# Local and global attention with a routed expert layer: the order of the first global keys, and who clears the padded values of V

## The chip, the cores and the metric

The kernel runs on one core of a Trainium2 chip. The metric is the device time of one execution in microseconds; the kernel before has a median of 1015.91 us over three runs (1014.29 to 1016.57). A core has five engines that work side by side, each through its own queue in order: TensorE (PE in the profile: matrix products and transposes), VectorE (DVE), ScalarE (ACT), GpSimd (POOL) and SyncE (SP, which here only issues transfers). ScalarE and GpSimd issue transfers too; on those engines an issue takes its turn in the same queue as their arithmetic. Engines wait for one another, and for transfers, by semaphores.

## The reference

Eight batches, eight heads, 512 local and 32 global tokens per head, 64 values each. Global tokens attend to everything; local tokens attend to the 32 global keys and to the local keys at most 32 places away. The attention output, 4352 tokens of 512 values, goes into a layer of eight experts whose weights per token come from a softmax that is balanced in eight rounds over rows and columns.

```python
k_all = np.concatenate([k_g, k_l], axis=2)
v_all = np.concatenate([v_g, v_l], axis=2)
out_g = np.matmul(sm(scale * q_g @ k_all^T), v_all)
mask  = np.abs(pos[:, None] - pos[None, :]) <= 32
s_ll  = np.where(mask, scale * q_l @ k_l^T, -1e9)
s_l   = np.concatenate([scale * q_l @ k_g^T, s_ll], axis=-1)
out_l = np.matmul(sm(s_l), v_all)
...
logits = x @ w_gate            # P: softmax, then 8 rounds of row and column sums
for e in range(E):
    out += P[:, e:e+1] * (np.maximum(x @ w1[e], 0.0) @ w2[e])
```

(The products are abridged here; `sm` is the softmax over the last axis.)

## The kernel before

The attention runs in 32 units: a unit is one batch and two of its heads (four units to a batch). The loop at line 497 takes steps s = 0, 1, 2, ...; at each step several units are in work at different stages, and the instructions of all engines are issued in exactly the order in which the code names them. Nothing is reordered: what stands in front on an engine's queue goes first.

The stages of a unit n are:

- st_A (line 279): transposes of its keys and queries on TensorE (line 287), then copies out of PSUM: keys to kTe[n % 4] by VectorE (line 289), queries by ScalarE (line 292 into qpl for the first six units, line 296 into the block-diagonal qbd after that).
- st_B (line 299), in three parts: the scores of local queries with the local keys in reach and with the batch's 32 global keys (lines 316, 319, 321), masked and reduced by VectorE (line 326), exponentials by ScalarE (line 329). The global keys are read from kgT.
- st_D1 and st_D2 (lines 332, 342): transposes of the probabilities, and of a finished unit's output into xT.
- st_E (line 359): the probabilities times V (line 372), then the division (lines 376, 377).
- st_G1 to st_G4 (lines 382 to 431): the same for global queries, two units at a time. They read qgT, kgT and kTe.

From step 5 on, first-layer and then second-layer products of experts 0 and 1 (p_l1, line 448, and p_l2, line 462) are put between these stages. After the attention the balancing and the other six experts follow; they fill the time from about 360 us to the end and are not touched.

V has three tiles per batch parity. va holds the local V in blocks of 128 rows, 65 values per head: 64 of V, and a 1 in column 64 (Dh), which makes the sum of probabilities come out with the product. vb holds the same shifted by 64 rows. vgz holds the 32 global rows four times, padded with zeros, so that a product of 128 rows picks the right 32. The zeros and ones are set once for each parity: clear (line 247) does a block of zero rows in va and the columns of ones in va and vb; clear_z (line 253) zeroes vgz and sets its ones. Batch 0 uses the tiles of parity 0, cleared by VectorE (lines 258, 261); batch 1 those of parity 1, cleared by GpSimd (lines 273, 274). Later batches find the padding in place.

V comes by load_v (line 161): GpSimd issues the global V into a scratch in DRAM (line 167), four loads of va (lines 168, 171) and one of vb (line 174). For batches 0 and 1 the rest of vb is built on GpSimd by five copies out of va (part, lines 176 to 183). load_vz (line 157) brings the global V from the scratch into vgz, issued by SP.

Ahead of the loop stand: the loads of batch 0's first heads and of four batches' global keys and queries (load_gf, line 205, on SP's and ScalarE's queues), more loads on GpSimd, the zeros and ones, the band mask (built by GpSimd at line 265, copied by VectorE at lines 490 to 493), st_A(0), then the global keys of four batches at once (cast_g and transpose_g, lines 212 and 217: one cast of 128 rows, four transposes, one copy into kgT), then st_A(1). In the loop: qgs is cast at step 0 and transposed at step 1; batch 1's V loads stand at step 2 (line 503), with load_vz(1) behind the first of them (line 526); qbd is cleared by GpSimd at step 3 (line 509); batch 2's Q and K (line 501), expert 1's w1, the copies that build batch 1's vb, and expert 0's w2 at step 4 (line 513); keep_busy (line 482) puts three and two products of no use into steps 1 to 4.

Of the kernel before, what the change touches and what calls it, by code (L numbers as in the profile page):

```python
# [10 lines left out]
FP16 = mybir.dt.float16  # L11
# [12 lines left out]
def kernel(  # L24
# [13 lines left out]
    nc = tc.nc  # L38

    B, H, Sl, Dh = q_l.shape  # L40
    Sg = q_g.shape[2]
    D, E = moe_w_gate.shape
    F = moe_w1.shape[2]
    P = 128
# [6 lines left out]
    HP = H // 2  # L51
# [17 lines left out]
    identity = persist.tile([P, P], FP16)  # L69
# [58 lines left out]
    with ExitStack() as att:  # L128
# [4 lines left out]
        ps_tr = att.enter_context(tc.tile_pool(name="ps_tr", bufs=2, space=PSUM))  # L133
# [4 lines left out]
        kgT = att_c.tile([P, HP, B * Sg], FP16)  # L138
        qgT = att_c.tile([P, HP, B * Sg], FP16)
        qbd = [att_c.tile([P, NHB, P], FP16, name=f"qbd{i}") for i in range(2)]  # L140
        kTe = [att_c.tile([P, W + Sl + W], FP16, name=f"kTe{i}") for i in range(4)]
# [15 lines left out]
        def load_vz(b):  # L157
            for i in range(4):
                nc.sync.dma_start(out=vgz[b % 2][W * i : W * (i + 1), i, :, 0:Dh], in_=vg16[b])
# [36 lines left out]
        gst = {}  # L196
# [8 lines left out]
        def load_gf(hf, tg, f, engs):  # L205
            src = k_g if tg == "kgs" else q_g
            fv = f.rearrange("p (h d) -> p h d", h=H)
            for bb, eng in enumerate(engs):
                eng.dma_start(out=fv[W * bb : W * (bb + 1)], in_=src[4 * hf + bb].rearrange("h s d -> s h d"))
            gst[(hf, tg)] = (att_in.tile([P, H, Dh], FP16, tag=tg, name=tg, bufs=1), fv)  # L210

        def cast_g(tg):
            t, fv = gst[(0, tg)]
            nc.vector.tensor_copy(out=t, in_=fv)
            gst[(0, tg)] = t

        def transpose_g(hf, tg):
            t = gst[(hf, tg)]
            pt = ps_tr.tile([P, HP, P], FP16, tag="tr")
            for hp in range(HP):  # L220
                nc.tensor.transpose(pt[:, hp, :], t[:, 2 * hp : 2 * hp + 2, :], identity)
            dst = kgT if tg == "kgs" else qgT
            nc.vector.tensor_copy(out=dst[:, :, P * hf : P * (hf + 1)], in_=pt)

        def run(steps):
            for f in steps:
                f()
# [3 lines left out]
        f0 = ypool.tile([P, NJ, D], FP32, tag="y", name="f0")  # L231
        fh = [f0[:, t, :].rearrange("p (h s d) -> p h s d", h=2, s=NJ) for t in range(2)]
        for h in range(2):
            for t, (src, eng) in enumerate(((q_l, nc.sync), (k_l, nc.scalar))):
                eng.dma_start(out=fh[t][:, h], in_=src[0, h].rearrange("(p s) d -> p s d", s=NJ))
        load_gf(0, "kgs", f0[:, 2, :], (nc.sync, nc.scalar, nc.sync, nc.scalar))
        load_gf(0, "qgs", f0[:, 3, :], (nc.sync,) * 4)
        steps = load_qk(0, 2, 4, H)
        run(steps[0:2])
# [7 lines left out]
        def clear(i, eng):  # L247
            va, vb = vab[i]
            eng.memset(va[0:W, 0], 0.0)
            eng.memset(va[:, :, :, Dh:VW], 1.0)  # L250
            eng.memset(vb[:, :, :, Dh:VW], 1.0)

        def clear_z(i, eng):
            eng.memset(vgr[i].bitcast(mybir.dt.uint32), 0)
            for j in range(4):
                eng.memset(vgz[i][W * j : W * (j + 1), j, :, Dh:VW], 1.0)

        clear(0, nc.vector)
        for t in range(2):
            (nc.vector.tensor_copy if t else nc.scalar.copy)(out=staged[0][t][:, 0:2], in_=fh[t])  # L260
        clear_z(0, nc.vector)
        for a in range(2):
            band = mask[HB * a : HB * (a + 1), 1, 0:KW]
            for base, m, c in ((0, -1, 1), (2 * W, 1, -1)):
# [2 lines left out]
        run(steps[2:4])  # L267
        *steps, move = load_v(0)
        part = move()
        steps[0]()  # L270
        load_vz(0)
        run(steps[1:])
        clear(1, nc.gpsimd)
        clear_z(1, nc.gpsimd)

        st = {}
        NPL = 6
# [204 lines left out]
        def keep_busy(n):  # L482
            pm = ps_mm.tile([P, 512], FP32, tag="mm", name="pm")
            for i in range(n):
                nc.tensor.matmul(pm, identity, kgT[:, :, 0:P], start=True, stop=True)

        queue = []
        NU = B * HP
        st_A(0)
        nc.vector.tensor_copy(out=mask[:, 0, 0:KW], in_=mask[:, 1, 0:KW])  # L490
        nc.vector.tensor_copy(out=mask[:, 2, 0:KW], in_=mask[:, 1, 0:KW])
        nc.vector.memset(mask[:, 0, 0:W], NEG)
        nc.vector.memset(mask[:, 2, 3 * W : KW], NEG)
        cast_g("kgs")
        transpose_g(0, "kgs")
        st_A(1)
        for s in range(NU + 2):
            b, hp = divmod(s, HP)
            if s < NU and b + 1 < B:
                if hp == 0:  # L500
                    queue = load_qk(b + 1, 0, 4, H)
                if hp == 2:
                    *loads, move = load_v(b + 1)
                    queue += loads
                if hp == 3:
                    if s == 3:
                        part = move()
                        for t in qbd:
                            nc.gpsimd.memset(t, 0.0)
                    else:  # L510
                        queue = [move] + queue
                if s == 4:
                    queue += [lambda: wts.__setitem__(1, [load_w1(1)]), lambda: part(nc.gpsimd, True),
                              lambda: part(nc.gpsimd, False), lambda: wts[0].append(load_w2(0))]
                if s == 5:
                    queue += [lambda: load_g(1, "kgs"), lambda: load_g(1, "qgs")]
                if s == 7:
                    queue += [lambda: wts[1].append(load_w2(1))]
                take = 0 if s == 0 else 2 if s >= 8 and hp < 2 else len(queue)
                if s == 1:  # L520
                    queue += [lambda: part(nc.gpsimd, True), lambda: part(nc.gpsimd, False), load_first]
                    take = len(queue)
                for i, f in enumerate(queue[:take]):
                    f()
                    if s == 2 and i == 0:
                        load_vz(1)
                queue = queue[take:]

            if 8 <= s < 8 + 4 * (E - 2):
                sums_load(s - 8)  # L530
            if 8 < s <= 8 + 4 * (E - 2):
                sums_form(s - 9)

            l1, l2 = [], []
            if s >= 5:
                pieces = range(4 * (s - 6) + 2, 4 * (s - 6) + 6)
                l1 = [(i // FT % 2, i // FT // 2, i % FT) if i >= 0 else None for i in pieces]
            if s >= 6:
                k, hf = divmod(s - 6, 2)
                if k >= 1:  # L540
                    l2 = [((k - 1) % 2, (k - 1) // 2, 2 * hf + i) for i in range(2)]
            n1 = n2 = 0

            def f1(eng):
                nonlocal n1
                if n1 < len(l1):
                    if l1[n1]:
                        p_l1(*l1[n1], eng)
                    n1 += 1

            def f2(eng):
                nonlocal n2
                if n2 < len(l2):
                    p_l2(*l2[n2], eng)
                    n2 += 1

            g_odd = s % 2 == 1 and 3 <= s <= NU + 1
            if g_odd:
                gb, gg = divmod((s - 3) // 2, 2)
            even = s % 2 == 0 and 2 <= s <= NU  # L560
            f1("a")
            if s < NU:
                st_B(s, 0)
            if even:
                st_G1(*divmod((s - 2) // 2, 2))
            if 1 <= s <= NU:
                st_D1(s - 1)
            if s == 3:
                st_E(1)
            if g_odd:  # L570
                st_G2(gb, gg)
            f2("a")
            if s < 7:
                st_B(s, 1)
            if 1 <= s < 5:
                keep_busy(3)
            if 1 <= s:
                st_D2(s - 1 if s <= NU else None, s - 2 if s >= 4 else 0 if s == 3 else None)
            if 7 <= s < NU:
                st_B(s, 1)  # L580
            f1("a")
            if 0 < s < 7:
                st_A(s + 1)
            if s == 4:
                st_D2(None, 1)
            if s == 0:
                cast_g("qgs")
            if s == 1:
                transpose_g(0, "qgs")
            f1("v")  # L590
            if s < NU:
                st_B(s, 2)
            if s + 1 < NU and s >= 7:
                st_A(s + 1)
            if s == 2:
                st_E(0)
            if 3 <= s <= NU:
                st_E(s - 1)
            f2("a")
            if s >= 6 and (s - 6) % 4 == 0:  # L600
                logits(NJ * ((s - 6) // 4), NJ)
            if g_odd:
                st_G3(gb, gg)
            if s == 8:
                transpose_g(1, "kgs")
                transpose_g(1, "qgs")
            if s == 18:
                st_G4(0)
            f1("v")
            if 1 <= s < 5:  # L610
                keep_busy(2)
# [451 lines left out]
```

## Time and profile before

| | us |
|---|---|
| median of three runs | 1015.91 (1014.29 to 1016.57) |
| the profiled execution | 1014.09 |
| its span, first instruction to last | 1012.3 |
| TensorE busy in the span | 992.0 |
| VectorE busy | 778.9 |
| ScalarE busy | 632.7 |
| GpSimd busy | 299.7 |

The profile is of one execution. Times in a timeline count from the start of the span. "Busy" leaves out issuing instructions and waits; a row of a timeline gives the start, the duration, the engine, the line, the operation, the tile written and the tiles read, and in square brackets how long the engine was idle ahead of it and what released it. The share by engine in the chain tells which work, followed back from the last instruction, each step waited for. The granted clock is 0.999 of full speed over the whole span.

The transfer engines are busy in nearly all of the first 60 us: their mean share in the first ten fortieths of the span is 90% or more.

### The profile page before, as it was taken

How to read it: one execution, taken by the hardware profiler on the slowest of the kernel's cores; microseconds unless marked ns; L12 is line 12 of the kernel's file. 1: busy time of each engine (PE TensorE's matmuls, PEld its weight loads, DVE VectorE, ACT ScalarE, POOL GpSimd, SP SyncE). 2: the span in 40 equal slices, each digit the busy share in tenths (PEclk: the TensorE clock that was granted, in tenths of full speed). 3: DMA queues.
4: the chain of work that ended last, by engine and by line, in shares of the span. 5: the costliest groups of instructions: out<-in, count | busy, mean ns of one | idle time of the engine just before them, and what ended most of it. 6: DMA issues, size and time to landing. Idle time of an engine off the chain costs nothing.

```text
span 1012.3 us, 22271 instructions
## 1 busy us (share of the span) xinstructions
PE 992.0 (98%) x8774; PEld 644.2 (64%) x8774; DVE 778.9 (77%) x1890; ACT 632.7 (63%) x1342; POOL 299.7 (30%) x364
## 2 busy tenths in 40 slices
PE   6899999999999999999999999999999999999998
PEld 4666566656565555666666666676767676766764
DVE  7876766666664664889999888997889999887885
ACT  5877777777774566765555555556765555555551
POOL 9658878868860112111111111111111111100000
PEclk9999999999999999999999999999999999999999
DMA  9999999979952297654443333565664533123043
GB/s 164 183 164 206 223 211 214 219 162 225 224 155 84 88 256 167 157 146 115 115 115 74 73 73 74 126 186 148 158 147 121 115 74 86 48 69 74 1 105 125
DMA packets 135881, 138.40 MB, mean 137 GB/s; under 512 B 54432, under 2 KB 107872, under 8 KB 133728
## 3 DMA queue, kind: packets, MB, share of 16 engines
q0 software_dynamic: 105696, 87.32, 49.6%
q1 hardware_dynamic: 29248, 49.28, 15.0%
q8 instruction: 68, 1.11, 0.4%
q10 hardware_dynamic: 832, 0.39, 0.1%
q14 instruction: 37, 0.30, 0.1%
HBM read 144.20 MB, written 39.58 MB: 182 GB/s over the span
## 4 chain that ended last, share of the span: by engine, by line
PE 94%; DVE 3%; ACT 1%; DMA 1%; issue 0%; ACTq 0%; DVEq 0%
PE z L787 29%; PE pa L882 17%; PE ph L455 12%; PE py L469 12%; PE pb L882 9%; PE pc L882 5%; PE po L372 1%; PE zp L853 1%; PE ptw L338 1%; PE sc L319 1%; PE pk L287 1%; DVE ms L326 1%; PE po L416 1%; PE tgx L348 1%; PE pq L287 1%; DMA f<-in_k_g_dram 1%
## 5 line engine op out<-in xcount | busy, mean ns | idle before, releaser
L787 PEld LDWEIGHTS <-hs 128*128 128x128 f16 x2264 | 220.8, 98 | 92.8 <-issue 1.1
L787 PE MATMUL z<-w2e,hs 128*128 128x256 f16 x1304 | 195.6, 273 | 0.9 <-DVE oy L821 0.9
L787 PE MATMUL z<-v,hs 128*128 128x256 f16 x960 | 144.0, 273 | 0.0
L455 PE MATMUL ph<-xT,w1e 128*128 128x512 f16 (+1 forms) x576 | 129.6, 367 | 2.0 <-DVE lg L444 1.4
L469 PE MATMUL py<-w2e,hT 128*128 128x512 f16 x544 | 128.2, 379 | 0.4 <-DVE hT L460 0.4
L808 ACT COPY z<-z 128x256 f32<-128x256 f32 x98 | 35.0, 357 | 141.7 <-PE z L787 141.7
L882 PEld LDWEIGHTS <-w1e 128*128 128x128 f16 x960 | 86.5, 97 | 57.4 <-issue 1.2
L882 PE MATMUL pa<-t,s 128*128 128x512 f16 x384 | 114.2, 379 | 0.2 <-ACT s L907 0.2
L703 POOL DMA_DIRECT2D w1e<-in_moe_w_dram x24 | 17.4, 732 | 303.8 <-PE pa L882 229.9
L329 ACT ACTIVATE Pu<-ms,mx 128x160 f16<-128x160 f32 x256 | 92.2, 424 | 19.3 <-DVE mx L326 16.6
L821 DVE SCALAR_TENSOR_TENSOR oy<-z,lg,oy 128x512 f32<-128x512 f32 x128 | 95.8, 749 | 7.4 <-ACT oy L826 5.2
L783 DVE TENSOR_TENSOR hs<-hs 128x512 f16<-128x512 f16 x224 | 94.9, 424 | 8.2
L886 DVE CUSTOM_DVE_ANT_0 hx<-pb,s 128x512 f16<-128x512 f32 x96 | 65.9, 687 | 39.7 <-ACT s L916 31.5
L326 DVE CUSTOM_DVE_ANT_0 ms<-sc,mask 128x160 f32<-128x160 f32 x256 | 70.0, 320 | 34.1 <-PE sc L321 32.4
L703 POOL DMA_DIRECT2D w2e<-in_moe_w_dram x24 | 19.8, 830 | 242.6 <-PE z L787 212.3
L898 ACT ACTIVATE hs<-pc 128x512 f16<-128x512 f32 x96 | 57.2, 596 | 52.7 <-PE pc L882 52.6
L455 PEld LDWEIGHTS <-w1e 128*128 128x128 f16 x576 | 53.9, 98 | 52.6 <-issue 2.9
L886 DVE CUSTOM_DVE_ANT_0 hs<-pb,s 128x512 f16<-128x512 f32 x96 | 65.9, 686 | 27.3 <-ACT s L916 26.9
L882 PEld LDWEIGHTS <-s 128*128 128x128 f16 x720 | 65.6, 98 | 29.9 <-issue 1.8
L469 PEld LDWEIGHTS <-hT 128*128 128x128 f16 x544 | 50.0, 98 | 51.9 <-issue 0.5
L460 DVE TENSOR_SCALAR hT<-ph 128x512 f16<-128x512 f32 x58 | 40.1, 692 | 47.7 <-PE ph L455 46.4
L916 ACT COPY s<-pa 128x512 f32<-128x512 f32 x102 | 59.8, 586 | 12.0 <-PE pa L882 0.7
(194 smaller groups left out, 1968.4 us busy)
## 6 DMA issues: line engine op xcount, KB each, us to landing
ys<-yd SPq DMA_DIRECT2D x68, 256.0 KB, 3.3
yd<-yst SPq DMA_DIRECT2D x16, 1024.0 KB, 5.7
pw<-in_moe_w_dram POOLq DMA_DIRECT2D x24, 512.0 KB, 10.0
kept<-psum POOLq DMA_DIRECT2D x24, 512.0 KB, 4.8
s<-kept POOLq DMA_DIRECT2D x12, 768.0 KB, 9.1
v<-kept POOLq DMA_DIRECT2D x12, 768.0 KB, 9.1
w1e<-in_moe_w_dram POOLq DMA_DIRECT2D x12, 512.0 KB, 5.5
w2e<-in_moe_w_dram POOLq DMA_DIRECT2D x12, 512.0 KB, 6.6
```

The source lines that it names most:

```text
L326: nc.vector.tensor_tensor_reduce(out=ms[:, ii, :], in0=sc[:, SW * ii : SW * (ii + 1)], in1=mask[:, mi, :], scale=-scale, scalar=BIG, op0=A ...
L329: nc.scalar.activation(out=d["Pu"][:, i, :], in_=ms[:, ii, :], func=AF.Exp, scale=-1.0, bias=d["mx"][:, i : i + 1])
L455: nc.tensor.matmul(ph[:, 0:n], wts[e][0][:, dk, P * fm : P * (fm + 1)], xT[:, dk, c0 : c0 + n], start=(dk == 0), stop=(dk == DP - 1))
L460: nc.vector.tensor_scalar(out=hT[:, fm, 0:n], in0=ph[:, 0:n], scalar1=0.0, scalar2=None, op0=ALU.max)
L469: nc.tensor.matmul(py, hT[:, fk, P * c : P * (c + 1)], wts[e][1][:, fk, :], start=(fk == 0), stop=(fk == FT - 1))
L783: nc.vector.tensor_tensor(out=o, in0=x, in1=y, op=op)
L787: nc.tensor.matmul(o, lhs[:, fk, :], rhs[:, fk, :], start=(first and fk == 0), stop=(fk == HF - 1), skip_group_check=True)
L821: nc.vector.scalar_tensor_tensor(out=o, in0=z, scalar=p, in1=o, op0=ALU.mult, op1=ALU.add)
L882: nc.tensor.matmul(o, lhs[:, dk, P * f : P * (f + 1)], rhs[:, dk], start=(first and n == 0 and dk == 0), stop=(dk == HD - 1), skip_group_c ...
L886: nc.vector._custom_dve(TENSOR_ADD_SAT, out=self.to(i, j), in0=self.of(ps), in1=self.of(s), s0=BIG, s1=0.0)
L898: nc.scalar.activation(out=self.to(0, 0), in_=self.of(self.pc), func=AF.Relu)
L916: nc.scalar.copy(out=self.pre3, in_=self.pa)
```

## The change

It has four parts.

1. The first scores need the global keys of batch 0 alone. A new function, first_keys, casts and transposes only those 32 rows, behind st_A(0) and ahead of the loop. The cast and the transposes of the whole kgs tile move to step 2 and fill only the remaining columns of kgT (transpose_g has a start column c0); those of qgs both stand at step 1. One of the four loads of global keys goes from ScalarE's queue to SP's.
2. The second unit's transposes and copies, st_A(1), move from ahead of the loop into step 0, behind the second part of its scores.
3. The copies of the mask move ahead of st_A(0). keep_busy reads kTe[0] instead of kgT, in the same shape.
4. clear_z(0) goes from VectorE to GpSimd, behind all loads of batch 0's V, with load_vz(0) behind it. clear(1), clear_z(1) and load_vz(1) go from ahead of the loop, and from the first of batch 1's V loads, to behind all of batch 1's V loads at step 2.

```diff
+        def first_keys():
+            t, fv = gst[(0, "kgs")]
+            nc.vector.tensor_copy(out=t[0:Sg], in_=fv[0:Sg])
+            pt = ps_tr.tile([P, HP, Sg], FP16, tag="tr")
+            for hp in range(HP):
+                nc.tensor.transpose(pt[:, hp, :], t[0:Sg, 2 * hp : 2 * hp + 2, :], identity[0:Sg, 0:Sg])
+            nc.vector.tensor_copy(out=kgT[:, :, 0:Sg], in_=pt)
-        def transpose_g(hf, tg):
+        def transpose_g(hf, tg, c0=0):
...
-            nc.vector.tensor_copy(out=dst[:, :, P * hf : P * (hf + 1)], in_=pt)
+            nc.vector.tensor_copy(out=dst[:, :, P * hf + c0 : P * (hf + 1)], in_=pt[:, :, c0:P])
...
-        load_gf(0, "kgs", f0[:, 2, :], (nc.sync, nc.scalar, nc.sync, nc.scalar))
+        load_gf(0, "kgs", f0[:, 2, :], (nc.sync, nc.scalar, nc.sync, nc.sync))
...
-        clear_z(0, nc.vector)
...
-        steps[0]()
+        run(steps)
+        clear_z(0, nc.gpsimd)
         load_vz(0)
-        run(steps[1:])
-        clear(1, nc.gpsimd)
-        clear_z(1, nc.gpsimd)
...
-                nc.tensor.matmul(pm, identity, kgT[:, :, 0:P], start=True, stop=True)
+                nc.tensor.matmul(pm, identity, kTe[0][:, 0:512], start=True, stop=True)
...
-        st_A(0)
         (four copies and memsets of the mask)
-        cast_g("kgs")
-        transpose_g(0, "kgs")
-        st_A(1)
+        st_A(0)
+        first_keys()
...
                 for i, f in enumerate(queue[:take]):
                     f()
-                    if s == 2 and i == 0:
-                        load_vz(1)
+                if s == 2:
+                    clear(1, nc.gpsimd)
+                    clear_z(1, nc.gpsimd)
+                    load_vz(1)
...
-            if 0 < s < 7:
+            if s < 7:
                 st_A(s + 1)
...
-            if s == 0:
-                cast_g("qgs")
-            if s == 1:
-                transpose_g(0, "qgs")
+            if s == 1 or s == 2:
+                cast_g("qgs" if s == 1 else "kgs")
+                transpose_g(0, *(("qgs",) if s == 1 else ("kgs", Sg)))
```

## The prediction

> **What bounds the kernel now.** I read the page first (busy shares, the chain that ended last), then the timeline of the first 60 us engine by engine, since the diff touches nothing later, then the landings of single loads, and last the order of the built programs.
>
> ```profile
> span 1012.3 us, 22271 instructions
> PE 992.0 (98%) x8774; PEld 644.2 (64%) x8774; DVE 778.9 (77%) x1890; ACT 632.7 (63%) x1342; POOL 299.7 (30%) x364
> PE 94%; DVE 3%; ACT 1%; DMA 1%; issue 0%; ACTq 0%; DVEq 0%
> ```
>
> The page: TensorE sets the end. From about 42 us on it rarely waits, and then only on work that TensorE itself has just released (scores, VectorE, transposes). So a delay of TensorE at 42 us reaches the end whole; a gain ahead of 42 us reaches it only if nothing at 42 us holds TensorE back.
>
> ```profile
> 4.93 0.93 DVE L254 MEMSET vgz<- 128x1040 uint32 x1 [0.16 <-issue]
> 8.41 0.61 PE L221 MATMUL pt<-identity,kgs 128*128 128x128 f16 x4 [2.52 <-DVE kgs L214]
> 9.94 0.31 PE L316 MATMUL sc<-kTe,qpl 64*64 64x128 f16 x2
> 14.55 1.46 PE L485 MATMUL pm<-kgT,identity 128*128 128x512 f16 x3
> 20.37 0.82 PE L485 MATMUL pm<-kgT,identity 128*128 128x512 f16 x3
> 42.00 0.22 PE L372 MATMUL po<-va,pw 128*64 128x65 f16 x1
> 42.01 0.22 PE L372 MATMUL po<-vb,pw 128*64 128x65 f16 x1
> 42.63 0.62 PE L416 MATMUL po<-vb,pgs 128*128 128x260 f16 x4
> ```
>
> TensorE's timeline (the first line is VectorE's): the first scores start at 9.94, behind the global keys and the second unit's transposes. At 42.00 stands st_E(4), the first reader of batch 1's va, vb and vgz; it runs without a wait. The two pm rows are equal work, at 14.55 and at 20.37, with different prices: TensorE is slow until somewhere between 16.2 and 17.9.
>
> ```profile
> 10.47 0.52 POOL L249 MEMSET va<- 32x520 f16 x1
> 11.05 0.24 POOL L250 MEMSET va<- 128x32 f16 x1
> 11.11 0.33 POOL L251 MEMSET vb<- 128x32 f16 x1
> 11.17 1.13 POOL L254 MEMSET vgz<- 128x1040 uint32 x1
> 12.36 0.83 POOL L256 MEMSET vgz<- 32x8 f16 x4
> 13.10 0.76 POOL L153 DMA_DIRECT2D qs<-in_q_l_dram  x1
> ...
> 25.93 0.61 POOL L174 DMA_DIRECT2D vb<-in_v_l_dram  x1
> 26.57 1.85 POOL L509 MEMSET qbd<- 128x1024 f16 x2
> 30.46 0.76 POOL L153 DMA_DIRECT2D qs<-in_q_l_dram  x1 [2.03 <-PE po L417]
> ...
> 34.23 0.61 POOL L178 COPY vb<-va 32x520 f16<-32x520 f16 x1
> ...
> 38.00 0.61 POOL L183 COPY vb<-va 64x520 f16<-64x520 f16 x1
> ```
>
> ```profile
> L174 POOL DMA_DIRECT2D vb<-in_v_l_dram x1: 607/607/607, 25.9 to 25.9; - x1
> DMA to landing us min/median/max: 8.6/8.6/8.6
> ```
>
> GpSimd's timeline and the landing of batch 1's last load of V. GpSimd's queue runs in order and holds, one behind another, batch 1's V loads (to 26.5), the clearing of qbd, batch 2's Q and K loads, w1e(1), and the five copies that build batch 1's vb, which end at 38.61. The V load issued at 25.93 lands 8.6 later, at 34.5; the va load issued at 25.0 lands by 34.3. The clears of batch 1's padded values ran from 10.47 to 13.1, long before those loads, and nothing on GpSimd stands still for V: the copies come to their turn at 34.23.
>
> **The change part by part.**
>
> *Start.* VectorE loses clear_z(0) ahead of the first scores (4.93 to 6.45). Its queue becomes: ks cast ends 4.77; four mask copies, 0.51 from 7.09 to 7.60, so to 5.3; kTe(0) copy when its transposes end (4.82 + 0.64 = 5.46), to 6.2; cast of batch 0's k_g. That load landed 4.4 after its issue at 1.66, at 6.1 (the four k_g: 4.4 to 5.5), so the cast (0.49, its free size is unchanged) ends at 6.7. The narrow transposes and copy have no row; from above the wide ones (0.61 + 0.42), from below nothing: scores at 6.7 to 7.8. I take 7.8, the nearest row: 2.1 earlier than 9.94. If k_g landed with the late ones (5.5), 1.1 of it is gone.
>
> *What pays that back.* st_A(1) now sits inside step 0: VectorE's kTe copy 0.69 enters between the scores, the qgs cast 0.45 leaves: +0.24 on VectorE; ScalarE's qpl copy 0.48 enters there too, and ScalarE's row of eleven exponentials (11.02 to 14.64) is the longer queue, so I count +0.5. Step 1: qgs cast ahead of its transposes, +0.45. Step 2: kgs cast 0.45, four transposes 0.41, copy 0.3 to 0.42, all ahead of VectorE's last two scores: +1.2. Together +2.15 against -2.1: at 42 us nothing is won, with bounds of -1.3 (the late casts hidden under other waits) and +1.1 (k_g late).
>
> *At nothing.* One k_g load goes from ScalarE's queue to SP's: one issue of 0.45, the q_g loads behind it are wanted only in step 1; ScalarE's next work waits for q_l anyway. keep_busy reads kTe[0] in the same shape (0.82 for three); st_A(4) rewrites kTe[0] only behind it. clear_z(0) on GpSimd takes 1.93 (11.17 to 13.10) where clear(1) and clear_z(1) took 2.63, so batch 1's Q and K are issued 0.7 earlier; load_vz(0) on SP waits for it until about 12.4 instead of 12.0. st_E(0) reads it at 22.8; these loads took 4.5 to 9.5. Without that slack a late vgz(0) would hold TensorE 1:1.
>
> *The clears of batch 1.* They go behind batch 1's V loads on the same queue. They write the ones columns of the very tiles that those loads fill, and in the order of the built program the second one (va's ones) waits for the four va loads and the third (vb's ones) for the vb load: the tracking does not see that columns 0 to 63 and 64 are apart. In the program before, these memsets wait for no load. So GpSimd stands from about 26 until 34.5 with everything behind it: vgz(1), qbd, four Q/K loads of batch 2, w1e(1), the copies to vb, w2e(0), the second kgs and qgs, V of batch 2; SP's load_vz(1) waits for it as well. By rows: vb's ones start at 34.53; from there to the end of clear_z, 11.11 to 13.10, 1.99: 36.52; qbd 1.85: 38.37; the next load at 38.4 instead of 30.46: all behind it is 7.94 later. (The 2.03 idle ahead of 30.46 is swallowed; its releaser was at 30.4.) L183 then ends at 46.55 instead of 38.61.
>
> st_E(4) wants that copy at its third column block, half way through its 32 matmuls, about 42.28. In-order TensorE stands there until 46.55: +4.27. If V lands 0.7 earlier, as the earlier issue would allow at best, +3.6; the loads were queued behind w1e(0) and Q/K, so not all 0.7 arrives. I take **+4.0**. A gain at the start doesn't alter it, since the 46.55 comes from loads and GpSimd alone: the start is worth 0 on this path, whatever it saves.
>
> Late next: load_vz(1) starts near 36.5 instead of 30.5; issue 2 plus 4.5 to 9.5 gives 43 to 48; its longest landing was one sent while w1e(1) was moving, and now nothing moves between 34.5 and 38.4, so I take it inside the 46.5. w1e(1) landed at 45.5 for a first use past 55.8; w2e(0) at 50.5 for 62.4; batch 2's vb at 68 for st_E(8) near 77. All have over 9 for a delay of 8, with TensorE itself 4 later: cost 0.
>
> Sum against the profiled execution (1014.09: span 1012.3 and 1.8 around it): 1014.09 + 4.0 = 1018.1. The median of the three runs lies 1.8 above that execution, so forecast **1019.9**.
>
> *A rule that could make it worse.* The row: three pm cost 1.46 at 14.55 and 0.82 at 20.37, a ratio of 1.78, and no idle of TensorE past 10 us exceeds 1.02, so the trace can't show what 4 us of idle does. The Trainium skill, TensorE: Matmul & The Clock Gate, section "What's actually happening", says that TensorE falls to half its clock after one idle window of about 3.4 us; the slow rows at the start agree, the fall no row here shows. By that rule the sum would be the first rival's 1022.4, without it 1019.9.
>
> **The rivals.**
>
> 1. *TensorE comes out of the stall slow.* It would idle 4 to 5 us. Behind st_E(4) the chain is TensorE's back to back from 42.6 to 45.4, then mostly VectorE to 47.3, then TensorE to 50.0. At 1.78 the first 2.8 cost 2.2 more, the next 2.7 another 2.1 if it stays slow that long (at the start it stayed slow some 8 us of work, from 8.4). With 2.5 to the forecast: 1022.4, to 1024 at worst. For: the two pm prices. Against: no row shows TensorE falling back once it is fast, though none has an idle a quarter as long. Chance 0.25.
>
> 2. *The clears don't hold st_E(4), and the start's gain stays: faster.* Place: va's and vb's ones on GpSimd. It decides if batch 1's V lands by 30.3 or GpSimd catches up 4 us. For: batch 0's V landed 7.0 after issue. Against: 8.6 to 9.3 here, and the queue behind is packed. Then 1015.9 - 2.1 = 1013.8. Chance 0.06.
>
> 3. *Half hidden: no change to tell.* V lands some 2 us earlier, as the four vgz(1) loads, which fell among it at 30.5 to 34.3, are gone, and a bit of the start's gain counts: +0 to +2, say 1017. Chance 0.08.
>
> **How the numbers follow.** Forecast (+3.2 to +4.8) 0.61, rival 1 0.25, rival 2 0.06, rival 3 0.08. About 0.2% (2.0 us) is what a measurement of this kernel can tell from no change. Faster 0.06, same 0.08, slower 0.86. The range leaves out rivals 2 and 3 and the end of rival 1: 1017.0 to 1023.0.
>
> **What would show it.** GpSimd's timeline: idle of some 8 us ahead of va's ones, released by a DMA of va or vb; L178's copies near 42 to 46.6. TensorE: an idle of about 4 us inside st_E(4), ended by GpSimd's vb. First scores near 7.8, but st_E(4) reached near 42. Rival 1: the first-layer matmuls (L455 before) right behind st_E(4) far above 1.9 for eight. Wrong if GpSimd shows no such idle, or if the copies end before st_E(4).

## The result and the profile after

The changed kernel is slower by about half a percent: 1019.52 us median of six runs (1017.82 to 1021.48) against 1014.71 (1013.75 to 1016.57) for the kernel before, also of six, taken beside it. The ratio is 1.0045 with a 95% interval of 1.0029 to 1.0060, so 2.9 to 6.1 us. The forecast was 1019.9 us. Its way to that number holds only in part, and the runs below show where. One execution, of a kernel of experiment 5, ran at a granted clock of 0.657 and took 1464.71 us; it is in no time and no ratio below.

The profiled execution of the changed kernel took 1019.63 us. Its page, the span, the busy times and the shares of the chain by engine:

```profile
span 1017.9 us, 22281 instructions
...
PE 994.7 (98%) x8778; PEld 645.4 (63%) x8778; DVE 779.2 (77%) x1887; ACT 633.3 (62%) x1342; POOL 301.6 (30%) x369
...
PE 94%; DVE 4%; ACT 1%; issue 1%; DMA 0%; ACTq 0%; DVEq 0%
```

TensorE is still the bound; the span grew by 5.6 us and its busy time by only 2.7. GpSimd's timeline around batch 1's V (start, duration, engine, line, operation, tiles; in brackets the idle time ahead and what ended it):

```profile
25.84 0.52 POOL L257 MEMSET va<- 32x520 f16 x1
33.34 0.25 POOL L258 MEMSET va<- 128x32 f16 x1 [6.98 <-DMA va<-in_v_l_dram]
33.46 0.28 POOL L259 MEMSET vb<- 128x32 f16 x1
...
35.38 1.85 POOL L512 MEMSET qbd<- 128x1024 f16 x2
37.16 0.76 POOL L153 DMA_DIRECT2D qs<-in_q_l_dram  x1
...
40.94 0.61 POOL L178 COPY vb<-va 32x520 f16<-32x520 f16 x1
...
44.71 0.62 POOL L183 COPY vb<-va 64x520 f16<-64x520 f16 x1
```

The landing of that last V load (issued at 25.17, so it was there at 33.4):

```profile
L174 POOL DMA_DIRECT2D vb<-in_v_l_dram x1: 625/625/625, 25.2 to 25.2; - x1
...
DMA to landing us min/median/max: 8.2/8.2/8.2
```

The predicted stop is there, 6.98 us ahead of va's ones and ended by a load of va; batch 2's loads are issued from 37.16 instead of 30.46, and the last copy into vb ends at 45.33 instead of 38.61, 6.7 later. TensorE's timeline of the same execution:

```profile
6.77 0.31 PE L321 MATMUL sc<-kTe,qpl 64*64 64x128 f16 x2
...
7.16 0.23 PE L321 MATMUL sc<-kgT,qpl 64*64 64x32 f16 x2
...
20.93 1.46 PE L490 MATMUL pm<-kTe,identity 128*128 128x512 f16 x3
...
24.65 0.40 PE L229 MATMUL pt<-identity,kgs 128*128 128x128 f16 x4 [1.35 <-DVE kgs L214]
...
46.05 0.22 PE L377 MATMUL po<-va,pw 128*64 128x65 f16 x1
46.05 0.22 PE L377 MATMUL po<-vb,pw 128*64 128x65 f16 x1
...
47.24 1.89 PE L460 MATMUL ph<-xT,w1e 128*128 128x512 f16 x8
```

The first scores start at 6.77 instead of 9.94. But st_E(4) is reached at 46.05, and no bracket stands at it: TensorE found vb ready, because it was itself 4.05 late (42.00 before). That is not what was forecast. Three of keep_busy's products (pm) still cost 1.46 at 20.93, where before they cost 0.82 at 20.37; TensorE stayed slow until about 22.6, and the kgs cast that step 2 now holds met it with another wait. Two copies on VectorE then came beside GpSimd's late clearing of qbd (35.38 to 37.23):

```profile
35.92 1.39 DVE L340 COPY Pl<-Pu 128x256 f16<-128x256 f16 x1
36.05 1.26 DVE L345 COPY pw<-ptw 128x1024 f16<-128x1024 f16 x1
```

The same two copies in the kernel before, and, in a second view, TensorE's first-layer products behind its st_E(4) and the scores that follow them:

```profile
32.94 0.56 DVE L335 COPY Pl<-Pu 128x256 f16<-128x256 f16 x1
33.08 0.68 DVE L340 COPY pw<-ptw 128x1024 f16<-128x1024 f16 x1
```

```profile
43.20 1.89 PE L455 MATMUL ph<-xT,w1e 128*128 128x512 f16 x8
44.92 0.22 PE L319 MATMUL sc<-kTe,qbd 128*128 128x128 f16 x1
```

So this execution was 2.98 late when the copies began, 3.81 late when the first ended and 3.55 when the second did. The question for the experiments was therefore whether the clears cost the time at all, or the start does.

### The profile page after: what moved, and what is told of

Read it like the earlier page. It is cut to its first block, busy times and chain, and to the rows that moved or that the text cites. A ratio compares the mean times of both kernels' runs of the same rounds, so it can differ in the third digit from the quotient of the medians.

```text
span 1017.9 us, 22281 instructions
## 1 busy us (share of the span) xinstructions
PE 994.7 (98%) x8778; PEld 645.4 (63%) x8778; DVE 779.2 (77%) x1887; ACT 633.3 (62%) x1342; POOL 301.6 (30%) x369
## 4 chain that ended last, share of the span: by engine, by line
PE 94%; DVE 4%; ACT 1%; issue 1%; DMA 0%; ACTq 0%; DVEq 0%
PE z L791 29%; PE pa L886 17%; PE ph L460 12%; PE py L474 11%; PE pb L886 9%; PE pc L886 5%; PE po L377 1%; PE zp L857 1%; PE sc L324 1%; PE ptw L343 1%; PE pk L292 1%; DVE ms L331 1%; DVE Pl L340 1%; PE tgx L353 1%; PE po L421 1%
```

## The experiments

All kernels compute the whole output; where products of no use are added, they only take time. Each time stands beside runs of the kernel before on the same chip.

**1. The start alone, the clears alone.** The first kernel is the changed one with batch 1's clears and load_vz(1) put back where they were:

```diff
         load_vz(0)
+        clear(1, nc.gpsimd)
+        clear_z(1, nc.gpsimd)
...
-                if s == 2:
-                    clear(1, nc.gpsimd)
-                    clear_z(1, nc.gpsimd)
-                    load_vz(1)
+                    if s == 2 and i == 0:
+                        load_vz(1)
```

> The changed kernel with the clears of batch 1 and load_vz(1) back where they were (ahead of the loop; behind the first load of batch 1's V). Two theories. Hold: GpSimd's stop for batch 1's V costs the 4.8 us, as forecast; without it the time is that of the kernel before, 1014.7, at most 1 us more. Start: the stop is hidden behind TensorE, which comes to st_E(4) at 46.0 by itself; only VectorE's two copies that ran beside GpSimd's clearing of qbd (0.7 late) and beside the vb copies (0.4) are won: st_E(4) near 45, 1017.5 to 1019, slower than before by 0.3 to 0.4%.

The second is the kernel before with nothing but the late clears:

```diff
-        clear(1, nc.gpsimd)
-        clear_z(1, nc.gpsimd)
...
-                    if s == 2 and i == 0:
-                        load_vz(1)
+                if s == 2:
+                    clear(1, nc.gpsimd)
+                    clear_z(1, nc.gpsimd)
+                    load_vz(1)
```

> The kernel before with one thing changed: the clears of batch 1 and load_vz(1) behind batch 1's loads of V. Hold: GpSimd stops for 7 to 8 us, the last copy of vb ends near 45 instead of 38.6, and TensorE, which was at st_E(4) at 42.0, stands there for about 3: +3, near 1017.7. If a late GpSimd costs nothing anywhere: +0 to +0.5, near 1015. Both theories of the first run agree with +3 here; only a chain through VectorE (copies beside the clearing of qbd, +1) could make st_E(4) late by itself.

The start alone: 1016.22 us (12 runs) against 1015.14, ratio 1.0011 [0.9999, 1.0024]. The clears alone: 1020.02 (6 runs), ratio 1.0050 [1.0037, 1.0063]. So the late clears carry all of the loss, in an order whose start is that of before. GpSimd's and TensorE's timelines of the kernel with the clears alone:

```profile
32.69 0.25 POOL L250 MEMSET va<- 128x32 f16 x1 [7.05 <-DMA va<-in_v_l_dram]
...
44.05 0.62 POOL L183 COPY vb<-va 64x520 f16<-64x520 f16 x1
```

```profile
41.30 0.22 PE L370 MATMUL po<-va,pw 128*64 128x65 f16 x1
44.16 0.19 PE L370 MATMUL po<-vb,pw 128*64 128x65 f16 x1 [2.63 <-POOL vb L182]
...
45.22 1.05 PE L414 MATMUL po<-vb,pgs 128*128 128x260 f16 x4
46.06 0.43 PE L415 MATMUL po<-vgz,pgs 128*128 128x260 f16 x1
46.28 2.85 PE L453 MATMUL ph<-xT,w1e 128*128 128x512 f16 x8
```

Here TensorE does stand inside st_E(4), for 2.63 us, until GpSimd's copy into vb (line 182; line 183 is met next, at 44.72). And behind it, it is slow: 1.05 for four products that took 0.62 before, 2.85 for eight that took 1.89. The granted clock (PEclk) of the same execution shows it, in stretches of 3.41 us:

```profile
core 0: us, PE busy (x) PEld busy (x) DVE busy (x) ACT busy (x) POOL busy (x), PEclk, DMA share, GB/s
41.39:44.80 3.41, 0.66 (x22) 0.43 (x24) 0.92 (x5) 1.10 (x3) 3.35 (x5) 1.00 1.27 162
44.81:48.22 3.41, 3.41 (x25) 1.84 (x25) 1.61 (x5) 0.61 (x2) 3.41 (x6) 0.50 1.14 210
48.23:51.64 3.41, 2.81 (x43) 1.91 (x42) 2.79 (x11) 2.06 (x5) 0.72 (x2) 1.00 1.18 208
```

TensorE ran at half clock from 44.81 to 48.22. The expected 1017.7 had the wait and not this, and was 2.3 us too low. In the kernel with the start alone nothing waits there:

```profile
41.77 0.22 PE L379 MATMUL po<-va,pw 128*64 128x65 f16 x1
...
42.40 0.62 PE L423 MATMUL po<-vb,pgs 128*128 128x260 f16 x4
...
42.96 1.89 PE L462 MATMUL ph<-xT,w1e 128*128 128x512 f16 x8
```

It reaches st_E(4) at 41.77 instead of 42.00, though its scores began 3 us earlier.

**2. The changed kernel once more.** If the route of the first profile (slow start, no wait) was that execution's and not the order's, a second profile of the unchanged kernel can show the other route.

> The changed kernel once more, one look. In its first profile TensorE stayed slow until 22.6, st_E(4) was reached at 46.05 and found the last copy of vb done at 45.3. Hold: the slow stretch is chance; where TensorE becomes fast earlier, it comes to st_E(4) near 42 and is stopped there until GpSimd's copies end near 45, and the end is the same, 1018 to 1020. Start: the slow stretch belongs to the changed order; TensorE is slow until 22 again and st_E(4) is reached at 46 without a stop.

It took 1019.94 us beside 1015.1. TensorE's timeline of this second execution:

```profile
17.04 0.60 PE L490 MATMUL pm<-kTe,identity 128*128 128x512 f16 x2
...
41.54 0.22 PE L377 MATMUL po<-va,pw 128*64 128x65 f16 x1
45.12 0.19 PE L377 MATMUL po<-vb,pw 128*64 128x65 f16 x1 [3.37 <-POOL vb L182]
...
45.69 0.21 PE L377 MATMUL po<-vb,pw 128*64 128x65 f16 x1
...
46.22 1.05 PE L421 MATMUL po<-vb,pgs 128*128 128x260 f16 x4
47.06 0.43 PE L422 MATMUL po<-vgz,pgs 128*128 128x260 f16 x1
47.28 2.61 PE L460 MATMUL ph<-xT,w1e 128*128 128x512 f16 x8
49.73 0.22 PE L324 MATMUL sc<-kTe,qbd 128*128 128x128 f16 x1
```

The two pm products at 17.04 cost 0.60 (1.03 at 17.24 in the first profile), so the same program became fast some 8 us earlier. It then reached st_E(4) at 41.54 and was held 3.37 us, as forecast, and came out slow (granted clock 0.50 from 45.32 to 48.74). Two executions of one order take two routes to nearly the same lateness: one loses the time at the start and meets a vb that is ready, the other is on time and waits for it. A route without a wait in one profile was no evidence that GpSimd cost nothing. How often an execution takes which route is not known from two profiles.

**3. What TensorE's speed behind the stop costs.** Twelve products of no use right ahead of st_E(4) keep TensorE at work for most of the stop:

```diff
+            if s == 5:
+                keep_busy(12)
             if 3 <= s <= NU:
                 st_E(s - 1)
```

> The changed kernel with twelve products of no use (128x512) right ahead of st_E(4), so that TensorE works through most of the stop there. In the second look at the changed kernel TensorE waited 3.4 at st_E(4), and then eight first-layer products took 2.61 instead of 1.89 and the value products 1.0 instead of 0.6. If TensorE falls back to slow because it stood still, it stays fast here: the eight products take 1.9, and the time is 1 to 2 us below the changed kernel, near 1018. If the slow stretch has another cause, 1019.5 to 1020.5.

```profile
41.28 2.76 PE L490 MATMUL pm<-kTe,identity 128*128 128x512 f16 x12
43.98 0.22 PE L377 MATMUL po<-va,pw 128*64 128x65 f16 x1
45.49 0.19 PE L377 MATMUL po<-vb,pw 128*64 128x65 f16 x1 [1.29 <-POOL vb L182]
...
46.40 0.62 PE L421 MATMUL po<-vb,pgs 128*128 128x260 f16 x4
...
46.97 1.89 PE L460 MATMUL ph<-xT,w1e 128*128 128x512 f16 x8
```

TensorE's timeline of this kernel: 1.29 us of idle is left, and the products behind it have the prices of before. The granted clock reads 1.00 from 41 to 50 us. The place is settled; on the whole time, where 1 to 2 us less were expected, it could not be told: 1019.35 (6 runs) against 1015.33, ratio 1.0041 [1.0026, 1.0056]. Its copies into vb also ended later in the profiled execution (fifth vb product at 46.05, against 45.69 in the second profile), which took back part of what the speed gave.

**4. Which clear makes the stop.** Only the zeros and ones of va and vb go back ahead of the loop; clear_z(1) and load_vz(1) stay late:

```diff
         load_vz(0)
+        clear(1, nc.gpsimd)
...
                 if s == 2:
-                    clear(1, nc.gpsimd)
                     clear_z(1, nc.gpsimd)
                     load_vz(1)
```

> The changed kernel with clear(1) alone back ahead of the loop; clear_z(1) and load_vz(1) stay behind batch 1's loads of V. The memsets of the ones then wait for no load, and GpSimd does not stop, though the work of clear_z(1) stays where the change put it. If the stop is the cause: GpSimd's copies end at 38 to 40, as before, no stop at st_E(4), 1014.5 to 1016.5 as in the first run. If the place of the work is the cause, waits or not: 1018 and more.

1015.80 (12 runs), ratio 1.0003 [0.9988, 1.0018]. GpSimd's timeline has no idle for V, and the chain behind it is early again:

```profile
26.66 0.97 POOL L262 MEMSET vgz<- 128x1040 uint32 x1
...
28.42 1.85 POOL L513 MEMSET qbd<- 128x1024 f16 x2
...
38.41 0.62 POOL L183 COPY vb<-va 64x520 f16<-64x520 f16 x1
```

TensorE's timeline shows what is late next once vb is not:

```profile
43.92 0.19 PE L378 MATMUL po<-vgz,pg 128*64 128x65 f16 x1 [1.13 <-DMA vgz<-vg]
```

This is load_vz(1), which stands behind clear_z(1). The unit's next scores come at 46.66 (44.92 before), and the lateness of 1.74 is still there at 78.38 (76.64 before). The interval of the whole time reaches to 1.0018, 1.8 us, so it neither shows nor excludes this. To take the wait of the ones away without moving them was not tried.

**5. Whether the start can be made to pay.** Four kernels tried to turn 3 us of earlier scores into time. The first fills TensorE's idle time in steps 0 to 2 of the start-alone kernel with products of no use:

```diff
             if s == 1 or s == 2:
+                keep_busy(2 if s == 1 else 4)
                 cast_g("qgs" if s == 1 else "kgs")
...
-            if 1 <= s < 5:
+            if s < 5:
                 keep_busy(2)
```

> The first run's kernel with products of no use in TensorE's waits: two at the end of step 0, two ahead of the cast of qgs in step 1, four ahead of the cast of kgs in step 2. In the changed kernel TensorE is slow until about 22.5 (three pm products 1.46 at 20.93), in the kernel before until about 17. If the waits in steps 0 to 2 keep it slow, it is fast by 18 here and st_E(4) comes 1.5 to 2 us earlier than in the first run: near 1016. If the waits have no part in it, the same as the first run or up to 0.5 later.

1015.82 (11 runs), ratio 1.0004 [0.9992, 1.0015]; no profile of it is read. The next are the kernel before, the changed kernel and the start-alone kernel with 30 small products of no use ahead of st_A(0) (the kernel before has 20 more behind it):

```diff
+        def warm(n):
+            pm = ps_mm.tile([P, 512], FP32, tag="mm", name="pm")
+            for i in range(n):
+                nc.tensor.matmul(pm[:, 0:P], identity, identity, start=True, stop=True)
+
+        warm(30)
         st_A(0)
```

> The kernel before with products of no use of the identity in TensorE's idle start: 30 ahead of st_A(0), 20 behind it. If steady work makes TensorE fast, it is fast by 10 instead of 17: the three pm products of step 1 take 0.82 instead of 1.46, and st_E(3) comes 1 to 2 us earlier. st_E(4) also waits for the last load of vgz(1), which landed at 42.0 in the kernel before, so the gain may stop there: 1013 to 1014.7. If work doesn't matter: 1014.7.

> The changed kernel with 30 products of the identity, of no use, ahead of st_A(0), which make TensorE fast from the start. Hold: TensorE comes to st_E(4) at 40 to 41.5, stops there until GpSimd's copies of vb end at 45 or a little later, and the time stays at 1018 to 1019.5. Start: with the slow stretch gone the loss is gone, 1014.5 to 1016.

> The first run's kernel (clears of batch 1 ahead of the loop) with the same 30 products. Both theories: no stop, TensorE fast throughout, st_E(4) at 40 to 41, 1013 to 1015, and less spread than the first run's 1014.2 to 1018.4, if that spread came from when TensorE became fast. If the spread has another source, it stays.

The kernel before with them: 1013.93, ratio 1.0001 [0.9983, 1.0019], with three of its twelve runs near 1020 (1019.85 to 1020.18); the changed kernel: 1021.89, 1.0058 [1.0039, 1.0076], above the expected range, and with st_E(4) reached no earlier than before (42.62); the start-alone kernel: 1015.86, 1.0009 [0.9993, 1.0025]. The last has not less spread than without the products (1014.25 to 1021.74, against 1014.18 to 1018.40), so the spread is not shown to come from the start. In the warmed kernel before the three pm products cost 0.82 at 14.20, as was meant. To see whether its runs near 1020 come again, it was run once more.

> The kernel before with products of the identity, of no use, ahead of st_A(0) (30) and behind it (20), once more, to see whether its three runs near 1020 of twelve come again. If they are its own: 1013.9 with some runs near 1020; if they were the chip's: 1013 to 1015 throughout.

1014.81, ratio 0.9997 [0.9986, 1.0008], the slowest of twelve runs at 1018.29. TensorE's row for the three pm products, first of the one execution and then of the other:

```profile
14.20 0.82 PE L485 MATMUL pm<-kgT,identity 128*128 128x512 f16 x3
```

```profile
14.45 1.46 PE L485 MATMUL pm<-kgT,identity 128*128 128x512 f16 x3
```

The same instructions, once fast and once slow: the early products make TensorE fast, but do not keep it so. In the slow one the granted clock falls to 0.50 at 11.06 and returns at 17.89; in the fast one it reads 1.00 throughout. In the other two warmed kernels it is 0.50 from 9.44 to 19.68 (changed; the three products cost 1.46 at 12.57) and from 7.76 to 14.59 (start alone; 1.46 at 12.37), though no idle time above 0.93 us lay between the 30 products and the fall.

The last takes away what would be late next in the start-alone kernel: batch 1's global V is loaded right behind batch 0's V, and load_vz(1) follows at once.

```diff
-                nc.gpsimd.dma_start(out=vg16[b], in_=v_g[b].rearrange("h g d -> g h d"))
+                if b != 1:
+                    nc.gpsimd.dma_start(out=vg16[b], in_=v_g[b].rearrange("h g d -> g h d"))
...
         clear(1, nc.gpsimd)
         clear_z(1, nc.gpsimd)
+        nc.gpsimd.dma_start(out=vg16[1], in_=v_g[1].rearrange("h g d -> g h d"))
+        load_vz(1)
...
-                    if s == 2 and i == 0:
-                        load_vz(1)
```

> The first run's kernel (clears of batch 1 ahead) with batch 1's global V loaded behind batch 0's V and vgz(1) filled at once, instead of behind expert 0's w1. In the run with only the ones ahead, st_E(4) waited 1.1 for vgz(1); in the one with the warm start 1.7. If that load is what TensorE meets next, no wait for vgz here, st_E(4) at 41.5 to 42: 1014 to 1015, below the first run's 1016.2. If it seldom decides, the same as the first run.

1016.50 (11 runs), ratio 1.0002 [0.9993, 1.0012]; st_E(4) is reached at 41.91 with nothing to wait for, but the time is not below that of the start alone, as it was expected to be. So no form of the start gained time that could be measured, and no kernel beats the kernel before. Nor does time won by 77 us have to reach the end: in the fast profile of the warmed kernel before the scores near 77 start at 75.61, 1.03 early, and its span is 1012.1, 0.2 shorter.

**All of them at four marks.** The starts of the same instructions on TensorE: the fifth vb product of st_E(4), which is the first that needs line 183's copy; the scores behind the eight first-layer products; the same scores three units on. "Behind the stop" is the second mark less the first, less the 2.64 (44.92 - 42.28) of before.

| kernel | st_E(4) reached | wait for vb | fifth vb product | scores | late | behind the stop | scores near 77 | late |
|---|---|---|---|---|---|---|---|---|
| before | 42.00 | 0 | 42.28 | 44.92 | | | 76.64 | |
| changed, first profile | 46.05 | 0 | 46.33 | 48.97 | 4.05 | 0 | 80.68 | 4.04 |
| changed, second profile | 41.54 | 3.37 | 45.69 | 49.73 | 4.81 | 1.40 | 81.44 | 4.80 |
| clears alone | 41.30 | 2.63 | 44.72 | 48.97 | 4.05 | 1.61 | 80.68 | 4.04 |
| changed, warmed | 42.62 | 2.87 | 46.27 | 50.60 | 5.68 | 1.69 | 82.31 | 5.67 |
| changed, stop filled | 43.98 | 1.29 | 46.05 | 48.69 | 3.77 | 0 | 80.41 | 3.77 |
| start alone | 41.77 | 0 | 42.05 | 44.69 | -0.23 | 0 | 76.40 | -0.24 |
| start alone, early global V | 41.91 | 0 | 42.19 | 44.83 | -0.09 | 0 | 76.55 | -0.09 |

What TensorE is late at 45 us it is late at 77, to 0.01 us. And the measured times divide by the stop: kernels whose GpSimd stops for V have ratios of 1.0041 and more, those without the stop 1.0011 and less. The lateness is not the whole growth of a profile, though. Against 1012.3 before, the spans of the five profiles with the stop are 5.0 to 7.7 longer, 1.0 to 2.0 more than their lateness near 77; those of the start alone, with early global V, and with the ones ahead are 0.4, 0.6 and 1.6 longer, which is 0.6 and 0.7 more and 0.1 less. No run was made to find what adds this behind 77 us.

## Why the prediction was right, and where it was wrong

*The bound, and that a delay at 42 us reaches the end whole: right.* The columns "late" at 45 and 77 us agree in every kernel, and no profile with the stop makes up for its lateness later. The difference of the medians, 1019.52 - 1014.71 = 4.81, is the size of the lateness in the second profile; that both are the same to the hundredth is chance, since more is added behind 77 us.

*The stop of GpSimd: right in place and cause, over in size.* The ones of va wait for the loads of va. The prediction had GpSimd back at 34.5; it was back at 33.34 (32.69 with the clears alone). V was issued 0.76 earlier (25.17 instead of 25.93) and landed after 8.2 instead of 8.6. The prediction saw the earlier issue and let it count for 0.27 of the 4.27; a shorter landing stands only in its rival 3. From vb's ones to the end of line 183's copy it reckoned 12.02 (34.53 to 46.55); 11.87 was measured (33.46 to 45.33). So the term that was mis-sized is the landing of V, by 1.1.

*The hold of TensorE, +4.0: too high.* Where TensorE was held (second profile), the fifth vb product came 45.69 - 42.28 = 3.41 late. TensorE had come 0.46 early (41.54), stood 3.37 for line 182's copy, and then shortly for line 183's. In the first profile the copies ended (45.33) before st_E(4) was reached (46.05): that is the sign by which the prediction would have been wrong, and there the lateness came by the other route.

*TensorE comes out fast: this step failed.* The forecast counted nothing for it and gave the slow exit to rival 1, with 2.5 us. It came out slow in all three profiled executions that were held 2.63 us or more, for 1.40, 1.61 and 1.69 us; with 1.29 us of idle time it came out fast. So rival 1's mechanism is part of the true cause, at 0.56 to 0.68 of its price: TensorE had half its clock for 3.41 us in each of the three, then the old prices. Half of 3.41 is 1.71, and up to 1.69 of it was lost; the rival reckoned with slow prices for longer. The first profile, where nothing was held, shows the other side: eight products at 1.89. The forecast's total is near because misses offset. By the second profile the hold was 0.6 less than +4.0, the slow exit 1.4 more than nothing, and the median of before, taken at 1015.91 from three runs, was 1014.71 over six, 1.2 less. Together -0.6 + 1.4 - 1.2 = -0.4: 1019.5 instead of 1019.9. That it comes out so near is luck: the first profile has neither of the first two terms, and the sum leaves out what is added behind 77 us.

The rule that was weighed there, from the Trainium skill, TensorE: Matmul & The Clock Gate, section "What's actually happening", is that TensorE drops to half its clock after an idle window of about 3.4 us. The fall itself agrees with the rows (granted clock 0.50; four products 1.05 instead of 0.62). The length does not, read as one unbroken idle stretch: 2.63 us was enough here, and the measurement decides. Nor were the 3.41 us ahead of the fall free of work: TensorE was busy for 0.66, 0.18 and 1.15 us of them. The page adds that the window runs freely and that the moment of warming varies from run to run, by 500 ns either way; the two executions of one program, fast some 8 us apart, agree that it varies, but by far more.

*The start, worth 0: right.* Its two terms stand in the start-alone kernel: scores about 3 us earlier, st_E(4) at 41.77, 0.23 earlier, within the bounds of -1.3 to +1.1, and no measurable gain at the end. The narrow transposes and their copy took 0.28 and 0.23, where the wide ones' 0.61 and 0.42 were taken; the gain was 2.96 instead of 2.1 (scores at 6.98) and the payback 2.73 instead of 2.15. In the first profile of the changed kernel, though, the start was not worth 0: that execution was 2.98 late when the two copies began, ahead of any read of vb.

*Late next, at nothing: right for the changed kernel, and only behind the stop.* load_vz(1) was not met in either profile. With the stop gone it is next, for 1.13 us in the kernel with the ones ahead.

*Rivals 2 and 3* (the clears hidden, or half hidden) are refuted by the kernel with the clears alone, at 1.0050.

*What stays open.* Why TensorE stayed slow until 22.6 in the first profile, beyond that it is the execution and not the order. In that profile the span is 5.6 longer but TensorE only 4.04 late at 77 us: the other 1.5 arises between 90 and 121 us, and no run was made for it; the six runs of the changed kernel spread over 3.7 us.

## What to carry to other kernels

A memset of padding columns into a tile that a load is filling can wait for the whole load, even where the bytes are apart; put it ahead of the load's issue, or look up its waits in the built order before putting it behind. Count what stands behind the waiting instruction on its queue, not the instruction: here a memset of 0.25 us held 12 us of GpSimd's work. And take a second profile of the same program before believing that a chain without a wait clears a suspect: where two routes to the same lateness run in parallel, one execution shows only one of them.

## What the hardware showed unexpectedly

Behind a stop TensorE ran at half clock for the same 3.41 us each time: the granted clock is 0.50 from 44.81 to 48.22 (clears alone), 45.32 to 48.74 (second profile) and 46.99 to 50.40 (changed, warmed), and 1.00 on both sides. It fell not at the end of the wait but 0.2 to 1.3 us behind it, so the first products behind the stop still had the old prices (the first two rounds of st_E(4) in the second profile, 0.19 to 0.22 each, against mostly 0.24 and 0.25 from 45.31 on). The length of a single idle time does not decide it: 2.63 us was enough, 1.29 was not, nor the 1.72 for which the warmed start-alone kernel waits for vgz (clock 1.00 from 41 to 50 us); but early in two warmed kernels it fell with no idle time above 0.93 us. What does decide it these runs don't show. At the very start the column of the granted clock reads 1.00 while equal products are slow (1.46 at 20.93 in the first profile), so there only the prices show it.

A copy on VectorE was held by GpSimd's two memsets of qbd in the first profile. Line 340's, which reads and writes SBUF, took 1.39 instead of 0.56 and ended at 37.31, right behind the memsets (37.23); line 345's, next on VectorE's queue, took 1.26 instead of 0.68 and ended with it. In the second profile, with no memset beside them, the same lines took 0.33 and 0.68 at 37.93. Not every 16-bit copy is held: in the kernel before, the copy out of PSUM into kTe took 0.69 at 27.76, its usual price, beside the same memsets (26.57 to 28.42). The Trainium skill, GPSIMD Engine Reference, section "Specifications", says that GpSimd shares its SBUF interfaces with VectorE and lists which VectorE instructions contend. The held copy agrees with the sharing; whether it is of a kind on that list no run shows.
